# Two real parts instead of three ahead of the first output of layer 0's channel transform

## The chip, the cores and the metric

The kernel runs on one core of one Trainium2 chip. The metric is the device time of one execution in microseconds (us); the time before is the median of three executions, 749.95 us. Beside the times there is one profiled execution with its trace. TensorE is called PE in the profile (its weight loads PEld), VectorE is DVE, ScalarE is ACT, GpSimd is POOL, and SP is the queue from which all of this kernel's DMAs are issued.

## What is computed

Two layers, each a Fourier mixing followed by a linear-attention block, on a 2048 x 640 matrix of 32-bit floats, each part with a layer norm ahead of it and a residual behind it.

```python
def _A_ref(x, dft_seq_re, dft_seq_im, dft_hid_re, dft_hid_im):
    a = jnp.einsum("bsd,ed->bse", x, dft_hid_re)
    b = jnp.einsum("bsd,ed->bse", x, dft_hid_im)
    return jnp.einsum("ts,bse->bte", dft_seq_re, a) - jnp.einsum("ts,bse->bte", dft_seq_im, b)

def _B_ref(x, wqkv, wo):            # B, S, D = 1, 2048, 640; 32 heads of 20
    q, k, v = split_heads(x @ wqkv)
    pq, pk = phi(q), phi(k)         # phi(t) = where(t > 0, t + 1, exp(t)) + 1e-6
    kv, z = pk^T v, sum(pk)         # per head
    return merge_heads((pq @ kv) / (pq . z + 1e-6)) @ wo

for layer in range(2):
    x = x + _A_ref(_layernorm(x), ...)
    x = x + _B_ref(_layernorm(x), B_wqkv, B_wo)
```

## The kernel before

**Tiles and precision.** The 2048 rows are 16 tiles of 128 rows, `X[0]` to `X[15]`, which stay in SBUF throughout. A product is made of three matmuls on a reduced-precision 32-bit type: each operand is split into a high part (a cast, on ACT, line L183) and a low part (source minus high part, line L184, on DVE or POOL), and high by high, high by low and low by high are added up in PSUM.

**The Fourier part.** The matrix is folded by its mirror symmetries, so that the sequence transform is made in classes. `Fourier.whole` (plan word `sCc`) makes one piece of a class: matmuls at L1061 and L1066, then the split of the result, the tiles `u`. The channel transform takes these as stationary operands: `hidden` makes one real or imaginary part of 128 rows from 9 matmuls of 322 columns (L1102). `Fourier.outputs(par, ahead, mid)` (plan word `oPA`) makes the four outputs `r` of one parity. Output `r` needs its real part `real(r)` and its imaginary part in one PSUM tile; `ahead` is the number of real parts that are written before the first imaginary one, and each output then gives out one more. An output is evacuated by ACT (`yi`, L1127 or L1129) and DVE (`ym` at L1130, `yp` at L1131), and four additions put it into two of the row tiles (`lo`, L1133 and L1134; `hi`, L1141 and L1142). The first output of even parity also has one special row, made by another `hidden` into a PSUM tile `p2` and copied at L1138 and L1139.

```python
    def outputs(self, par, ahead, mid=None):
        ...
        for r in range(ahead):
            real(r)
        for r in range(4):
            p = pu[r]
            self.hidden(2 * par + 1, 128 * r, p, 512)
            if r == 0 and mid is not None:
                mid()
            ...                      # yi, ym, yp and the additions into lo
            if par == 0 and r == 0:
                p2 = k.psum()
                self.hidden(0, 512, p2, 0)
            ...                      # the additions into hi
            real(r + ahead)
```

**The plan of layer 0.** `PLANS[0]` is a list of words that are worked through in order by `Fourier.work`: the odd outputs (`o11`), six pieces of classes, `w` (the key weights: five loads into `raw`, five splits into ten tiles `w`), `b` (the first layer norm of the attention, `xn0`, made at L177), `q` (the query weights, five more loads and splits), and `o03t`: the even outputs with three real parts ahead, where the `t` puts `Attention.begun` in as `mid`. `begun` transposes `xn0` on PE (five matmuls, L196, into a PSUM tile) and splits it into `x0` (L183 on ACT, L184 on DVE), which is the stationary operand of the first key and query projections (L245). `keys_values` follows: a loop over the 16 row tiles with one key and one query projection each.

**Buffers.** There are four PSUM tiles of two banks each, taken in turn by real parts, `begun`, `p2` and the projections, 12 buffers `tmp` (the channel weights take six of them, and `xn0`, `x0`, `yi`, `ym`, `yp` come from it too), 4 buffers `raw` for weights and for the tiles `ck` of a check of the input matrices, and 31 buffers for `u`, `w` and others.

**What sets the order.** In this stage the order of instructions on PE, ACT, DVE and POOL is not written by hand. A planner takes at compile time, from the instructions that are ready in its own view of time, the one with the highest priority: the place in the program, moved by the table `AHEAD`. There the query weights' splits have a head start of 200 places (`'0w0': 200`), the evacuation of even output 0 is put back by 600 (`'0out00': -600`), and that of even output 3 is put ahead by 600 (`'0out03': 600`). Each engine then works through its list in order, each instruction waiting for its operands and its buffer. The DMA queue keeps the order of the program. Within `keys_values` the planner also places the steps of the check (L1230, DVE); in the later outputs of layer 0's attention the order is written by hand.

Of the kernel before, what the change touches and what calls it, by code (L numbers as in the profile page):

```python
# [56 lines left out]
ASTATS = ((4, 10, 11, 13, 14), (1, 4, 8, 10))  # L57
VSTATS = ((4, 7, 13), (1, 2, 6, 7, 8, 13, 15))
RESID = ((4, 4), (3, 3))
PLANS = ('o11 s11 s12 s02 s00 s01 s10 w b q o03t', 's00 o12 s11 s12 s10 s01 s02 b w q o01t')  # L60
COL = (0, 1, 3, 2)
WLOWS = ((4, 0), (1, 1))
PAUSES = (4, 10, 11, 12, 13, 14)
# [955 lines left out]
class Fourier:  # L1019
# [141 lines left out]
    def run(self, T, att):  # L1161

        self.work(T, att, PLANS[self.k.layer])

# [370 lines left out]
```

## Time and profile before

| | us |
|---|---|
| median of three executions (749.91 to 750.39) | 749.95 |
| the profiled execution | 750.25 |
| its span in the trace | 748.1 |
| PE busy in the span | 726.5 |
| PE weight loads busy | 690.3 |
| DVE busy | 585.1 |
| ACT busy | 374.5 |
| POOL busy | 248.9 |

The span is what the trace covers from its first to its last instruction; the profiled execution was 2.15 us longer than that. Busy times of different engines overlap. Matmuls are pipelined, and a busy PE counts the modelled length of each, so two of them overlap in part. The granted TensorE clock is 1.00 throughout. In the timeline, a row has the start, the length, the engine, the line, the operation, output and input with their shapes and the count; what stands in brackets is how long the engine was idle ahead of it and what it had waited for.

### The profile page before, as it was taken

Reading aid. Unit: us, or ns where it says so; the run is one execution under the profiler, and the core shown is the slowest. Engines: PE = TensorE matmul, PEld = TensorE weight load, DVE = VectorE, ACT = ScalarE, POOL = GpSimd, SP = SyncE. Lnnn points to the kernel's source line nnn. Section 1 sums busy time; section 2 is a strip of 40 time slices with the busy share of each in tenths; the row PEclk is TensorE's granted clock in tenths of the full one; section 3 lists DMA queues with packets and bytes.
Section 4 is the critical chain, followed back from the end, with each engine's and each line's share of the span. In section 5 each row is a group of like instructions: output and inputs, shape, how many; then the busy total and the mean of one; then the engine's idle time right before and its main releaser. Section 6 shows DMA issues by size and latency. Waiting matters only on the chain.

```text
span 748.1 us, 12737 instructions
## 1 busy us (share of the span) xinstructions
PE 726.5 (97%) x4734; PEld 690.3 (92%) x4734; DVE 585.1 (78%) x1142; ACT 374.5 (50%) x705; POOL 248.9 (33%) x282
## 2 busy tenths in 40 slices
PE   4999999999999999999999999999999999999997
PEld 1388999999999999899986999999999999989997
DVE  7997798758968786888984756966887886689983
ACT  7745655664355543455773336566532554443320
POOL 5237932120014002567773672026000020154300
PEclk9999999999999999999999999999999999999999
DMA  9322467445665840400043222645265535002553
GB/s 335 97 90 90 128 201 257 126 133 181 187 187 184 283 146 21 151 9 1 11 140 133 70 94 77 222 144 168 59 187 168 164 114 155 23 12 71 178 171 114
DMA packets 55548, 98.78 MB, mean 132 GB/s; under 512 B 5268, under 2 KB 22935, under 8 KB 55479
## 3 DMA queue, kind: packets, MB, share of 16 engines
q1 hardware_dynamic: 55479, 97.89, 41.2%
q8 instruction: 39, 0.64, 0.4%
q14 instruction: 30, 0.25, 0.1%
HBM read 75.84 MB, written 21.63 MB: 130 GB/s over the span
## 4 chain that ended last, share of the span: by engine, by line
PE 80%; DVE 10%; ACT 6%; issue 2%; DMA 1%; POOL 1%; SPq 0%; DVEq 0%; ACTq 0%
PE ps L245 50%; PE ps L338 18%; PE ps L1156 4%; PE ps L1102 4%; PE ps L520 2%; PE ps L196 1%; DVE t L184 1%; PE ps L1061 1%; DVE w L184 1%; ACT t L885 1%; DVE ps L586 1%; DVE x L615 1%; ACT t L886 1%; ACT ab L922 1%; ACT ab L923 1%
## 5 line engine op out<-in xcount | busy, mean ns | idle before, releaser
L245 PE MATMUL ps<-w,t 128*128 128x320 f32 x2880 | 432.4, 310 | 0.5 <-DVE w L184 0.2
L245 PEld LDWEIGHTS ps<-w,t 128*128 128x128 f32 x2880 | 422.9, 188 | 2.0 <-DVE t L184 0.4
L338 PE MATMUL ps<-t,t 128*128 128x256 f32 (+1 forms) x640 | 139.9, 309 | 0.0
L1230 DVE CUSTOM_DVE_ANT_0 junk<-ck,ck 128x688 bf16<-128x688 f32 (+5 forms) x138 | 103.6, 751 | 7.5 <-DMA ck<-in_ck 5.7
L338 PEld LDWEIGHTS ps<-t,t 128*128 128x128 f32 x640 | 106.9, 188 | 0.0
L338 PE MATMUL ps<-w,t 128*128 128x384 f32 (+1 forms) x320 | 98.6, 310 | 0.7 <-DVE w L184 0.6
L370 ACT ACTIVATE t<-ps 128x640 f32<-128x640 f32 x64 | 45.1, 704 | 96.3 <-PE ps L245 96.2
L183 ACT CAST t<-t 128x640 fp32r<-128x640 f32 x62 | 45.2, 728 | 68.7 <-DVE t L213 41.1
L570 POOL TENSOR_TENSOR t<-pq,t 128x640 f32<-128x640 f32 x26 | 42.5, 1642 | 106.4 <-ACT t L488 77.3
L407 POOL TENSOR_TENSOR t<-t,s 128x640 f32<-128x640 f32 x16 | 28.4, 1772 | 130.1 <-DVE s L373 123.5
L338 PEld LDWEIGHTS ps<-w,t 128*128 128x128 f32 x320 | 60.2, 188 | 1.4 <-DVE w L184 1.3
L184 DVE TENSOR_TENSOR t<-t,t 128x640 fp32r<-128x640 f32 x52 | 43.3, 833 | 19.5 <-ACT t L183 11.7
L1102 PE MATMUL ps<-t,u 128*128 128x322 f32 x306 | 48.1, 315 | 1.1 <-DVE t L184 1.1
L1102 PEld LDWEIGHTS ps<-t,u 128*128 128x128 f32 x306 | 46.0, 189 | 2.2 <-issue 1.3
L372 ACT ACTIVATE t<-t 128x640 f32<-128x640 f32 x64 | 47.5, 742 | 0.0
L373 DVE SCALAR_TENSOR_TENSOR pq<-t,pq 128x640 f32<-128x640 f32 x32 | 27.6, 863 | 23.9 <-ACT t L372 23.9
L373 DVE SCALAR_TENSOR_TENSOR s<-t,s 128x640 f32<-128x640 f32 x32 | 26.9, 842 | 20.4 <-ACT t L372 20.4
L184 POOL TENSOR_TENSOR t<-t,t 128x640 fp32r<-128x640 f32 x10 | 16.2, 1620 | 71.9 <-ACT t L183 71.8
L183 ACT CAST t<-ps 128x640 fp32r<-128x640 f32 (+1 forms) x36 | 24.8, 690 | 27.2 <-PE ps L196 23.5
L183 ACT CAST t<-s 128x640 fp32r<-128x640 f32 x32 | 23.3, 728 | 29.5 <-DVE t L184 17.4
L1156 PE MATMUL ps<-cw,ab 128*128 128x512 f32 x80 | 35.6, 595 | 1.4 <-ACT ab L922 1.0
L184 DVE TENSOR_TENSOR t<-ps,t 128x640 fp32r<-128x640 f32 (+1 forms) x36 | 29.2, 812 | 7.9 <-ACT t L183 7.9
(198 smaller groups left out, 987.3 us busy)
## 6 DMA issues: line engine op xcount, KB each, us to landing
ck<-in_ck SPq DMA_DIRECT2D x48, 346.0 KB
ck<-in_ck SPq DMA_DIRECT2D x48, 344.0 KB
turn<-t SPq DMA_DIRECT2D x23, 320.0 KB
save<-w SPq DMA_DIRECT2D x20, 320.0 KB
w<-save SPq DMA_DIRECT2D x20, 320.0 KB
z<-turn SPq DMA_DIRECT2D x19, 320.0 KB
x<-in_x SPq DMA_DIRECT2D x16, 320.0 KB
out<-x SPq DMA_DIRECT2D x13, 320.0 KB
```

Source lines behind the costliest of these rows:

```text
L183: self.nc.scalar.copy(hi, src)
L184: return self.engine(pool).tensor_tensor(lo, src, hi.bitcast(F32), op=ALU.subtract)
L245: nc.tensor.matmul(pu[:m, 512 * h : 512 * h + HD], s, w[:, HD * h : HD * h + HD], start=first, stop=last)
L338: nc.tensor.matmul(self.place(G, c, part), x[:, 128 * c : 128 * c + 128], p[:, f : f + n], start=start and i == 0, stop=stop and i == 2, s ...
L370: nc.scalar.activation(h2(e), halves(pu), AF.Relu, scale=-1.0)
L372: nc.scalar.activation(e, e, AF.Exp, scale=-1.0)
L373: k.ve.scalar_tensor_tensor(out, e, 1e-6, out, op0=ALU.add, op1=ALU.add)
L407: k.engine(n not in PKSUMS[k.layer]).tensor_tensor(pksum, pksum, pk, op=ALU.add)
L570: k.behind(k.nc.gpsimd.tensor_tensor(t1, self.PQ[self.order2[n]], self.zb, op=ALU.mult), lull)
L1102: self.k.nc.tensor.matmul(po[:, o : o + 322], s[:, f : f + 128], w[:, x, :], start=start, stop=stop)
L1156: self.k.nc.tensor.matmul(self.sum(j), T.out["o", q][:, 128 * j : 128 * j + 128], self.C[2, g], start=n == 0, stop=n == 3)
L1230: i = nc.vector.tensor_tensor_reduce(k.junk[:, : a.shape[1]], b, a, 1.0, 0.0, op0, op1, o)
```

## The change

The word `o03t` of layer 0's plan becomes `o02t`: two real parts are written ahead of the first imaginary part, in place of three. The third real part is then written after output 0 (and `p2`), and the fourth after output 1. Nothing is added or left out: the same matmuls, transposes, evacuations and loads are made, in another order of the program, which the planner starts from.

```diff
-PLANS = ('o11 s11 s12 s02 s00 s01 s10 w b q o03t', 's00 o12 s11 s12 s10 s01 s02 b w q o01t')
+PLANS = ('o11 s11 s12 s02 s00 s01 s10 w b q o02t', 's00 o12 s11 s12 s10 s01 s02 b w q o01t')
```

## The prediction

> **What bounds the kernel now.** I read the page first, then who made PE wait around the changed stage, then that stage in order of time on each engine, then the stage after it.
>
> ```profile
> span 748.1 us, 12737 instructions
> ...
> PE 726.5 (97%) x4734; PEld 690.3 (92%) x4734; DVE 585.1 (78%) x1142; ACT 374.5 (50%) x705; POOL 248.9 (33%) x282
> ...
> PE 80%; DVE 10%; ACT 6%; issue 2%; DMA 1%; POOL 1%; SPq 0%; DVEq 0%; ACTq 0%
> ```
>
> PE is busy for 97% of the span and carries 80% of the chain that ended last. The change neither adds nor removes an instruction, so a gain can only be a pause of PE that goes away, and a loss only a pause that comes. The waits of PE between 30 and 140 us are two, and one of them lies in the stage that the change reorders:
>
> ```profile
> PE ps L1102 <- DVE t L184: 1.1, 1, 1.1
> PE ps L1156 <- ACT ab L922: 0.2, 1, 0.2
> ```
>
> The timeline of PE there:
>
> ```profile
> 63.66 5.89 PE L1102 MATMUL ps<-t,u 128*128 128x322 f32 x37
> 69.38 0.71 PE L196 MATMUL ps<-ident,t 128*128 128x128 f32 x5
> 69.85 2.78 PE L1102 MATMUL ps<-t,u 128*128 128x322 f32 x17
> 73.69 4.29 PE L1102 MATMUL ps<-t,u 128*128 128x322 f32 x27 [1.06 <-DVE t L184]
> 77.93 6.26 PE L245 MATMUL ps<-w,t 128*128 128x320 f32 x41
> ```
>
> A part is 9 matmuls, and the last 27 take 77.93 - 73.69 = 4.24 us, so 0.157 us for one and 1.41 for a part. There are nine parts, 81 matmuls. The counts (37, 17, 27, one record put into the neighbouring group) read as four parts, the transposes of `begun`, two parts, a pause of 1.06, three parts. With the four PSUM tiles this can be named: real 0, 1, 2 and the transposes fill all four (imaginary 0 goes into the tile of real 0); then only imaginary 1 and 2 have a place; then `p2`, real 3 and imaginary 3 wait until one tile comes back. The bracket says which: the one that the split of `x0` gives back (L184). Why so late is seen on ACT, DVE and POOL:
>
> ```profile
> 64.55 2.61 ACT L183 CAST w<-raw 128x640 fp32r<-128x640 f32 x4
> 69.72 0.73 ACT L183 CAST w<-raw 128x640 fp32r<-128x640 f32 x1 [2.57 <-DMA raw<-in_wqkv]
> 71.36 0.73 ACT L183 CAST w<-raw 128x640 fp32r<-128x640 f32 x1 [0.91 <-DMA raw<-in_wqkv]
> 72.00 0.69 ACT L183 CAST t<-ps 128x640 fp32r<-128x640 f32 x1
> 72.58 0.73 ACT L183 CAST w<-raw 128x640 fp32r<-128x640 f32 x1
> 73.21 0.43 ACT L1129 COPY t<-ps 128x322 f32<-128x322 f32 x1
> ...
> 65.83 3.02 DVE L184 TENSOR_TENSOR w<-raw,w 128x640 fp32r<-128x640 f32 x4
> 70.48 0.82 DVE L184 TENSOR_TENSOR w<-raw,w 128x640 fp32r<-128x640 f32 x1 [1.63 <-ACT w L183]
> 72.72 0.82 DVE L184 TENSOR_TENSOR t<-ps,t 128x640 fp32r<-128x640 f32 x1 [1.41 <-ACT t L183]
> 73.67 0.49 DVE L1130 TENSOR_TENSOR t<-ps,t 128x322 f32<-128x322 f32 x1
> ...
> 72.17 4.86 POOL L184 TENSOR_TENSOR w<-raw,w 128x640 fp32r<-128x640 f32 x3 [3.98 <-DMA raw<-in_wqkv]
> 76.99 1.12 POOL L1134 TENSOR_TENSOR x<-x,t 128x319 f32<-128x319 f32 x1
> ```
>
> The transposes are over at about 70.1, but their cast starts at 72.00: it stands in ACT's list behind the fifth and sixth weight cast, and the sixth waits 0.91 us for its load. Then DVE subtracts (72.72 to 73.54), and PE goes on at 73.69. Output 0's own evacuation stands still later, at 73.21 on ACT.
>
> **The change part by part.**
>
> *The order on PE.* Real 0, real 1 and imaginary 0 now come first. By the first group (36 matmuls in 69.38 - 63.66 = 5.72 us) these 27 end at 67.95, and the transposes at about 68.4, both 1.4 us sooner than before. Their source `xn0` is there by then:
>
> ```profile
> 64.64 0.61 DVE L177 TENSOR_SCALAR t<-x,kept 128x640 f32<-128x640 f32 x1 [0.65 <-POOL kept L158]
> ```
>
> Only three PSUM tiles are held at 68.4, so `p2` has the fourth without a wait (to 69.83), and imaginary 1 follows into the tile of real 1 (to 71.24). From there PE needs a tile given back: 71.24 is the new deadline, with two parts of cover behind the transposes as before, but both of them 1.4 us sooner.
>
> *What meets the deadline.* The stage cut at the gaps of ACT:
>
> ```profile
> 67.20:69.70 2.50, 2.50 (x19) 2.49 (x18) 1.65 (x3) 0.00 (x0) 0.99 (x2) 1.00 0.79 241
> 69.70:72.70 3.00, 2.93 (x21) 2.66 (x19) 0.82 (x1) 2.06 (x4) 0.53 (x1) 1.00 0.79 254
> 72.70:77.90 5.20, 4.21 (x27) 4.06 (x27) 5.05 (x9) 3.67 (x7) 5.20 (x4) 1.00 0.58 181
> ```
>
> Columns are stretch, length, then busy time (and instructions) of PE, PEld, DVE, ACT, POOL. From 67.20 to 69.70 ACT does nothing: it waits for the load of the fifth weight tile. Imaginary 0 (67.95) and the transposes (68.4) end inside that hole. The copy of output 0 (0.43) and the cast of the transposes (0.69) fit into it, to about 69.3; DVE, idle from 68.85 to 70.48, then needs 0.82 for the split or two times 0.49 for output 0, so that a tile is free between 69.9 and 70.7, ahead of 71.24. It hinges on the list: the planner must put this cast ahead of the fifth weight cast, or at least the sixth. In the list of before it stands behind the sixth and ahead of the seventh, although the query weights have the higher priority; so in the planner's view the seventh load was not there when the cast was ready, and the sixth was. Ready 1.4 us sooner, against 71.36 - 69.72 = 1.64 us between the fifth and sixth casts on the chip, it most likely moves up by at least one place. Behind the fifth only, it would end at 71.15 and the split at 72.0: a pause of 0.8 in place of 1.06. Ahead of the fifth, no pause. I take no pause, 1.06 us off, since output 0's copy, ready at 67.95, fills the same hole.
>
> *The bound of that term.* The trace's pause of 1.06 is counted from the modelled end of a matmul.
> The Trainium skill (Perfetto Trace Analysis, Identifying the Most-Contended Engine) says that the busy share of matmuls is a poor measure, since they are pipelined, and that of the weight loads a better one.
> By that rule the gain would be 1.3 us, as the next row shows, and the sum lower by 0.24.
>
> ```profile
> L1102 PEld LDWEIGHTS ps<-t,u 128*128 128x128 f32 x81 | 12.2, 190 | 1.3 <-issue 1.3
> ```
>
> I keep 1.06 and use 1.3 as the lower end.
>
> *What is late next.* Without the pause the nine parts end at 76.87 in place of 77.93, and the first key projection starts there. It needs ten weight tiles (the fifth pair was there at 71.3) and a PSUM tile; real 0, the transposes, real 1 and `p2` come back by then, and real 2 and 3 take two of them. So this start is covered. The second key projection is closer:
>
> ```profile
> 81.36 1.74 ACT L171 ACTIVATE t<-x,nb,kept 128x640 f32<-128x640 f32 x2 [2.91 <-POOL x L1142]
> 86.35 0.81 DVE L184 TENSOR_TENSOR t<-ps,t 128x640 fp32r<-128x640 f32 x1
> 84.88 15.84 PE ps L245 x108
> ```
>
> From the chain's row, 108 matmuls take 15.84 us, 0.147 each; the first query has 18 left at 84.88, so the second key starts at 87.52, and its operand is split at 86.35 + 0.81 = 87.16. The margin is 0.36. Ahead of that split ACT stood idle 2.91 us for a buffer that POOL's addition at L1142 gave back. If POOL's list stays as it is, PE keeps 0.36 of the 1.06 and waits the rest here; if output 0's additions go into POOL's own hole (the 3.98 us ahead of 72.17), they give buffers back over 1 us sooner, and all 1.06 stays. I take the middle, 0.7.
>
> *The rest.* No DMA is issued in the moved code, so the queue's list is as before; its loads into `raw` may start sooner or later with the splits that give the buffers back. POOL's list holds the last split of a query weight and its predecessors (1.62 us each, 4.86 for three), among which output 0's additions may now stand:
>
> ```profile
> 78.07 2.17 POOL L184 TENSOR_TENSOR w<-raw,w 128x640 fp32r<-128x640 f32 x1
> 63.25 0.73 DVE L184 TENSOR_TENSOR u<-ps,u 128x512 fp32r<-128x512 f32 x2
> ```
>
> The first row ends at 80.24; the first query, 30 matmuls of 0.147 behind 76.87, starts at 81.3 and still finds it, with 1 us of cover. The second row is the last large split of a class ahead of the stage, over at 63.98, while imaginary 0 now starts two parts behind 63.66, at 66.5.
>
> **Sum.** 750.25 for the profiled execution, less 0.7, is 749.55; the median of the runs is 0.30 below the profiled execution, so 749.25, given as 749.3. Its own range is 748.6 (1.3 off, all kept) to 750.0 (nothing kept). A measurement of this kernel tells about 0.2%, 1.5 us, from no change; so this forecast is no change.
>
> **The rivals.**
>
> *The split stays behind the sixth cast.* Then the tile comes back at 73.69 as before, but PE runs out at 71.24: a pause of 2.45 in place of 1.06, 1.39 us more, 751.3. For it: the query weights' head start in the priorities. Against it: the empty stretch of ACT above.
>
> *The lists behind the stage change (the slower side).* Key and query projections, check steps and splits are put in order by the same planner, which now starts from other times. The place is DVE in the key loop, which has no slack in its first stretch:
>
> ```profile
> 100.00:120.00 20.00, 20.00 (x139) 20.00 (x139) 19.22 (x37) 11.00 (x18) 2.57 (x4) 1.00 0.88 268
> L1230 DVE CUSTOM_DVE_ANT_0 junk<-ck,ck 128x688 bf16<-128x688 f32 (+5 forms) x138 | 103.6, 751 | 7.5 <-DMA ck<-in_ck 5.7
> ```
>
> A check instruction takes 0.751 us. One that newly stands ahead of a split for which PE is due costs about that, once the margin (0.36 above) is used. One undoes the gain of 0.7; three net make it slower by over 0.2%; five give 5 x 0.751 - 0.7 = 3.06, so 753.0; eight give 755.3. For it: DVE is busy for 19.22 of 20 us, and PE hardly waits in this loop now, so there is more to lose than to win. Against it: where DVE has a backlog, its order follows priorities rather than small shifts of time, and these are unchanged.
>
> *The lists change for the better.* The waits of PE in the whole run on splits:
>
> ```profile
> PE ps L245 <- DVE t L184: 1.9, 3, 1.5
> PE ps L245 <- DVE w L184: 1.0, 2, 0.8
> PE ps L338 <- DVE w L184: 0.6, 1, 0.6
> ```
>
> Together 3.5 us. Half of them gone and 0.7 from the stage would be 2.45 off, 747.5.
>
> *The change does nothing.* The planner might place real 2 ahead of imaginary 0 all the same, since it takes what is ready: 749.95. Against it: imaginary 0 now comes first in the program, and its operand is split 2.5 us before (the row above).
>
> **How the numbers follow.** Forecast 0.37, split behind the sixth cast 0.13, lists worse 0.37, lists better 0.09, nothing 0.04. Faster by over 0.2% is the better lists and a little of the forecast's lower end: 0.10. Slower is most of the worse lists (0.35) and 0.05 of the late split, which lies at the bound: 0.40. The rest, 0.50, is within 0.2%. The likeliest case gives 749.3. The range 748.0 to 755.0 takes in the forecast's own range, the late split and up to seven check instructions; outside lie half of the better lists and the tail of the worse, some 0.13.
>
> **What would show it.** Right: PE's first group at L1102 has 27 matmuls, the transposes stand near 68; on ACT the copy at L1129 and the cast of the transposes come ahead of the fifth or sixth weight cast; no wait of PE on L184 stands between 63 and 77, and the first projection starts near 76.9. If the second key starts at 87.5 as before, the margin took the gain. The late split shows as one pause of 2.4 us near 71. The worse lists show as new waits of PE at L245 or L338 between 90 and 320 us, and the prediction is wrong if these, or PE waits in the second layer, sum to over 2 us.

## The result, and the profile after

The median went from 750.2 us to 747.75 us: a ratio of 0.9971, with a 95% interval of 0.996 to 0.9981. That is 2.45 us, 0.29%, just beyond the 0.2% that a measurement here can tell. A second comparison gave 747.42 us and 0.9961 (0.9946 to 0.9976). The forecast was 749.3 us, within 0.2% of no change, with a range from 748.0: the right side and the right pause, but too small a gain, and 0.25 us below the range. The profiled execution took 747.61 us, against 750.25 before.

The page of the kernel after: span, PE's busy time, the chain.

```profile
span 745.8 us, 12737 instructions
...
PE 725.0 (97%) x4734; PEld 689.2 (92%) x4734; DVE 586.4 (79%) x1142; ACT 374.5 (50%) x705; POOL 246.9 (33%) x282
...
PE 16%; DVE 1%; ACT 0%; issue 0%; ACTq 0%
```

The same number of instructions is done in 2.3 us less. The chain's line is not comparable with the one before: here it could be followed back through 17% of the span only. PE's timeline in the changed stage after (start, length, engine, line, what, count):

```profile
63.42 3.05 PE L1102 MATMUL ps<-t,u 128*128 128x322 f32 x18
66.31 0.71 PE L196 MATMUL ps<-ident,t 128*128 128x128 f32 x5
66.77 9.67 PE L1102 MATMUL ps<-t,u 128*128 128x322 f32 x63
76.28 6.29 PE L245 MATMUL ps<-w,t 128*128 128x320 f32 x42
```

No row has a bracket: the pause is gone. The first group has 18 matmuls, two parts, so the transposes stand behind real 1 and *ahead* of imaginary 0, earlier than forecast. From the first part to the first key projection it is 76.28 - 63.42 = 12.86 us, where it was 14.28 (63.66 to 77.93, before rounding). ACT and DVE after:

```profile
64.32 2.61 ACT L183 CAST w<-raw 128x640 fp32r<-128x640 f32 x4
67.11 0.69 ACT L183 CAST t<-ps 128x640 fp32r<-128x640 f32 x1 [0.18 <-PE ps L196]
70.20 0.73 ACT L183 CAST w<-raw 128x640 fp32r<-128x640 f32 x1 [2.40 <-DMA raw<-in_wqkv]
70.84 0.42 ACT L1129 COPY t<-ps 128x322 f32<-128x322 f32 x1
...
68.55 0.81 DVE L184 TENSOR_TENSOR t<-ps,t 128x640 fp32r<-128x640 f32 x1
70.97 0.82 DVE L184 TENSOR_TENSOR w<-raw,w 128x640 fp32r<-128x640 f32 x1 [1.60 <-ACT w L183]
```

The cast of the transposes now runs at 67.11, ahead of the fifth weight cast, which waits 2.40 us for its load. So the split ends at 68.55 + 0.81 = 69.36. PE, with imaginary 0, `p2` and imaginary 1 behind the transposes (27 matmuls of (76.28 - 66.77) / 63 = 0.151 us), comes to the next part at 66.77 + 4.08 = 70.85 and finds the tile.

The orders of instructions of PE, DVE, ACT and POOL differ between the two kernels only inside this stage and the first key and query projections; the queue's order is the same, and nothing behind was put in another order. Between 80 and 110 us the weight loads of after wait twice, where those of before have no wait:

```profile
PEld ps L245 <- DVE t L184: 0.3, 1, 0.3
PEld ps L245 <- ACT t L183: 0.2, 1, 0.2
```

They belong to the second key projection. The rows of its operand after:

```profile
80.47 1.74 ACT L171 ACTIVATE t<-x,nb,kept 128x640 f32<-128x640 f32 x2 [2.29 <-DVE t L1131]
...
84.94 0.69 ACT L183 CAST t<-ps 128x640 fp32r<-128x640 f32 x1
...
86.31 0.81 DVE L184 TENSOR_TENSOR t<-ps,t 128x640 fp32r<-128x640 f32 x1
```

It is split at 87.12, as late as before (87.16), while PE now comes to it earlier.

Cut at the same instructions, the traces read as in this table (us, worked out from starts in PE's timeline before rounding). The cuts are the first even part, the first key projection, the transposes of the third operand, the first matmul of the Gram products (L520) and layer 1's first at L1156. "Again" is another execution of the same kernel in another comparison.

| stretch | before | before again | after | after again | one real part ahead | one, again | after, three POOL splits |
|---|---|---|---|---|---|---|---|
| up to the first even part | 63.66 | 63.40 | 63.42 | 63.67 | 63.66 | 63.49 | 63.39 |
| changed stage | 14.28 | 14.53 | 12.86 | 12.86 | 13.08 | 13.08 | 12.86 |
| first two keys | 22.62 | 22.57 | 23.09 | 23.55 | 22.49 | 22.49 | 22.50 |
| up to L520 | 192.83 | 192.57 | 192.34 | 192.54 | 192.47 | 192.74 | 192.47 |
| up to layer 1's L1156 | 94.16 | 94.13 | 93.81 | 93.82 | 94.29 | 94.30 | 93.85 |
| the rest | 360.51 | 360.83 | 360.26 | 360.04 | 360.59 | 360.66 | 360.18 |

By the means of two executions each, before and after, the stage gives 1.55, the first keys take back 0.72, and three later stretches, in which no instruction was moved, give 0.26, 0.33 and 0.52. So the moved instructions account for 0.8 us, less than half of the gain.

### The profile page after: what moved, and what is told of

Its sections match the earlier page's. It is cut to its first block, busy times and chain, and to the rows that moved or that the text cites. A ratio compares the mean times of both kernels' runs of the same rounds, so it can differ in the third digit from the quotient of the medians.

```text
span 745.8 us, 12737 instructions
## 1 busy us (share of the span) xinstructions
PE 725.0 (97%) x4734; PEld 689.2 (92%) x4734; DVE 586.4 (79%) x1142; ACT 374.5 (50%) x705; POOL 246.9 (33%) x282
## 5 line engine op out<-in xcount | busy, mean ns | idle before, releaser
L1156 PE MATMUL ps<-cw,ab 128*128 128x512 f32 x80 | 35.6, 595 | 2.2 <-ACT ab L923 1.4
L158 POOL TENSOR_TENSOR kept<-ve,mhalf 128x1 f32<-128x1 f32 x32 | 21.8, 699 | 41.4 <-DVE ve L157 40.1
```

The costliest lines, as they stand in the source:

```text
L1156: self.k.nc.tensor.matmul(self.sum(j), T.out["o", q][:, 128 * j : 128 * j + 128], self.C[2, g], start=n == 0, stop=n == 3)
```

## The experiments

Theory 1: the pause is a shortage of the four PSUM tiles, and it goes when the tile of the transposes comes back before PE runs out. Rivals: it goes only through the sooner split, whatever the number of parts; or only through the number of parts; or the gain is not in this stage at all.

**The transposes first, three parts ahead.** In layer 0 the order of the program becomes `begun`, then imaginary 0; three real parts stay ahead.

```diff
-            self.hidden(2 * par + 1, 128 * r, p, 512)
-            if r == 0 and mid is not None:
-                mid()
+            first = [mid] if r == 0 and mid is not None else []
+            for step in (first + [lambda: self.hidden(...)])[:: -1 if k.layer else 1]:
+                step()
```

> Three real parts ahead as before the change, but in the program the transposes of the first operand stand ahead of imaginary part 0 (layer 0 alone). The instruction lists differ from those before the change in this stage alone; the cast of the transposes moves up by one place, between the fifth and the sixth weight cast. Theory 1 (the split of the transposes comes too late on ACT): PE has imaginary 0, 1 and 2 as cover, to about 72.6 us, and the split is done at about 72.0; the pause of 1.06 us goes, first key projection 1.2 to 1.4 us sooner, time 748.5 to 749.1. Rival 1 (what counts is that one real part less holds a PSUM tile, so that p2 has one): four tiles are held as before, the pause stays, 750.2. Rival 2 (what counts is that output 0 is evacuated sooner): output 0 is no sooner here, 750.2.

Measured: 749.74 us, ratio 0.9984 (0.9973 to 0.9995); the profiled execution, 751.33 us, was the slowest of its twelve. Its PE timeline:

```profile
68.24 0.71 PE L196 MATMUL ps<-ident,t 128*128 128x128 f32 x5
68.71 5.18 PE L1102 MATMUL ps<-t,u 128*128 128x322 f32 x33
74.26 2.93 PE L1102 MATMUL ps<-t,u 128*128 128x322 f32 x18 [0.37 <-ACT t L1129]
77.58 6.40 PE L245 MATMUL ps<-w,t 128*128 128x320 f32 x42 [0.39 <-DVE t L1131]
...
89.35 0.86 PE L245 MATMUL ps<-w,t 128*128 128x320 f32 x4 [1.01 <-DVE t L184]
```

The wait for the split in the stage is gone, but two others stand in its place, for the tiles of the first outputs (L1129, L1131), and the second key waits 1.01 us. The stage is 14.02 us, 0.26 shorter than before. A sooner split alone moves the wait to the next tile: my expectation, the whole pause gone and 748.5 to 749.1 us, fell.

**Two parts ahead, the transposes late.** The change, with each matmul of `begun`'s transposes in layer 0 tied behind the last matmul of imaginary 0, which is the order that the prediction had assumed (the diff is shown in part). PE's timeline then has 29 matmuls ahead of them, the 27 of these parts and two more.

```diff
-        self.x0 = self.k.split_chunks(self.k.transposed(self.xn0))
+        tp = self.k.transposed(self.xn0)
+        [self.k.behind(t, self.k.last) for t in self.k.tps if self.k.part == 0 and not self.k.general]
+        self.x0 = self.k.split_chunks(tp)
```

> Two real parts ahead as after the change, but the transposes are tied behind the last matmul of imaginary part 0, where the program has them. In the lists the cast of the transposes falls back by one place, behind the fifth weight cast. Theory 1: PE has p2 and imaginary 1 as cover, to about 71.1 us; the fifth weight cast ends at 70.9, so the cast at 71.6 and the split, behind that weight's split on DVE, at 72.6; a pause of 1.2 to 1.8 us comes back, 749.0 to 749.7. Rival 1 (one real part less) and rival 2 (output 0 sooner): both are as after the change, 747.8 within 0.3.

Measured: 749.9 us, ratio 0.9987 (0.9976 to 0.9998). PE and ACT:

```profile
67.91 0.71 PE L196 MATMUL ps<-ident,t 128*128 128x128 f32 x5
68.38 2.64 PE L1102 MATMUL ps<-t,u 128*128 128x322 f32 x16
72.09 5.66 PE L1102 MATMUL ps<-t,u 128*128 128x322 f32 x36 [1.07 <-DVE t L184]
...
69.72 0.73 ACT L183 CAST w<-raw 128x640 fp32r<-128x640 f32 x1 [2.84 <-DMA raw<-in_wqkv]
70.35 0.69 ACT L183 CAST t<-ps 128x640 fp32r<-128x640 f32 x1
```

This is the prediction's hinge, on the chip. The transposes are over near 68.6, when ACT has nothing to do, yet their cast stands in the list behind the fifth weight cast and waits with it for the load. The pause is back with 1.07 us, and the stage has 14.20 us. The transposes' place on PE, behind 29 matmuls (67.91) or behind 18 (66.31), decides on which side of that cast the planner puts this one. The pause came out shorter than I expected (1.2 to 1.8), and the time still above the 749.0 to 749.7 that I gave.

**Three parts ahead, the cast on DVE.** The kernel before, with the high part of the transposes made by DVE in place of ACT; the orders of PE, POOL and the queue stay. The flag `on_dve` is set for layer 0's `begun` alone (lines left out here).

```diff
-        self.nc.scalar.copy(hi, src)
+        (self.nc.vector.tensor_copy if self.on_dve else self.nc.scalar.copy)(hi, src)
```

> Before the change, but the cast of the transposes (layer 0 alone) is made by DVE, right ahead of its subtraction, in place of ACT; the lists of PE, POOL and the DMA queue are those before the change, ACT's lacks the one cast. Theory 1: the split waits for no load of the sixth weight any more; cast and subtraction stand behind the fifth weight's split on DVE (ends at 71.3), so done at about 72.9 in place of 73.54: the pause falls from 1.06 to about 0.4, 749.5. Rivals 1 and 2: PE's order and output 0's are unchanged, 750.2 within 0.2.

Measured: 749.51 us, ratio 0.9984 (0.9972 to 0.9996). PE and DVE:

```profile
69.28 7.15 PE L1102 MATMUL ps<-t,u 128*128 128x322 f32 x44
77.14 6.40 PE L245 MATMUL ps<-w,t 128*128 128x320 f32 x42 [0.70 <-ACT t L1129]
...
69.54 0.83 DVE L184 TENSOR_TENSOR w<-raw,w 128x640 fp32r<-128x640 f32 x1 [1.26 <-ACT w L183]
70.28 0.82 DVE L183 CAST t<-ps 128x640 fp32r<-128x640 f32 x1
```

The cast no longer stands behind the sixth weight cast; on DVE it still follows the split of the fifth weight. The pause at the split is gone, of which I had expected 0.4 us to stay; but 0.70 us turns up ahead of the first key, which waits for a tile that ACT's copy of an output gives back. The stage is 14.05 us. So ACT's list was the reason for *that* wait, and with three parts ahead the next tile is nearly as late. The time is the 749.5 us that I expected, by another wait than I expected.

**One real part ahead.** `o03t` becomes `o01t`.

> One real part ahead of the first output in place of two. The transposes come on PE behind the first 9 matmuls, the cast behind the second weight cast. Theory 1: there is no pause left to win, the split only comes still sooner; the transposes want the normalised row tile at 65.0, just when PE comes to them, so 0 to 0.4 us may be lost: 747.7 to 748.3. Rival 1 (each real part less gives a gain): another 1 us off, 746.7. Rival 2 (output 0 sooner): it is sooner by one part, up to 0.6 off since buffers come back sooner ahead of the second key projection, 747.2.

Measured: 748.69 us, ratio 0.998 (0.9967 to 0.9992), and in a second comparison 748.21 us, 0.9971 (0.9962 to 0.998). PE:

```profile
63.66 1.70 PE L1102 MATMUL ps<-t,u 128*128 128x322 f32 x9
65.38 0.74 PE L196 MATMUL ps<-ident,t 128*128 128x128 f32 x5
65.87 11.03 PE L1102 MATMUL ps<-t,u 128*128 128x322 f32 x72
76.74 6.28 PE L245 MATMUL ps<-w,t 128*128 128x320 f32 x42
```

There is no pause here either. The stage is 13.08 us, 0.22 longer than with two, since 9 matmuls last until 65.1 and the source of the transposes is made by DVE only near 65.2 (64.64 + 0.61 in the row of L177, before). The first keys take 22.49 us: no loss there. By the moved instructions alone two would thus have no advantage over one: 0.22 in the stage, less the 0.60 to 1.06 that the stretch of the first two keys costs it. The medians say otherwise. In the comparison with both, one took 748.21 us and two 747.42, and the difference lies in the later stretches. The first measurement was above the 747.7 to 748.3 us that I expected.

**Both kernels again.** Before against itself: 750.25 us, ratio 1.0001 (0.999 to 1.0013).

> The kernel before once more, against itself, to see what of the difference between the two traces is the change and what differs from one execution to the next. If the stretches outside the changed stage (the start, 0.24 us; the fold behind layer 0's attention, 0.35 us; the second layer) differ by the execution, this trace shows differences of 0.2 to 0.5 us there and the stage itself at 14.3 us again (first even part to first key projection); ratio 1.000 within 0.001.

> The kernel after once more. Theory 1 (the stage alone): the stage takes 12.9 us again in place of 14.3, the second key projection loses 0.5 to 0.6 again, about 0.4 of that is won back at the first Gram product, and nothing else repeats: 1.4 us off, ratio 0.9981. Rival (the change also makes later stretches shorter): the fold behind the attention is 0.35 shorter again, ratio 0.997.

> One real part ahead, once more, beside the kernel after on the same chip. Theory 1: the stage takes 13.1 us, 0.2 more than with two, as PE reaches the transposes before their row tile is normalised, but nothing is lost at the second key projection, since the split of the second operand came 1.5 us sooner; from the stage to the third operand's transposes 0.4 us less than with two, so a ratio 0.0005 below that of the kernel after. Rival (what the first look showed): 0.0009 above it.

The pause in the second execution of before, with ACT's sixth weight cast, and then the stage and the third operand in the second execution of after:

```profile
73.69 4.28 PE L1102 MATMUL ps<-t,u 128*128 128x322 f32 x27 [1.32 <-DVE t L184]
...
71.37 0.73 ACT L183 CAST w<-raw 128x640 fp32r<-128x640 f32 x1 [1.28 <-DMA raw<-in_wqkv]
```

```profile
67.02 9.67 PE L1102 MATMUL ps<-t,u 128*128 128x322 f32 x63
76.53 6.29 PE L245 MATMUL ps<-w,t 128*128 128x320 f32 x42
...
PE ps L196 <- DVE t L177: 0.9, 1, 0.9
```

The same kernel's pause reads 1.06 in one execution and 1.32 in another. The rows say why: the sixth weight cast, which waits for its load, starts at 71.36 and 71.37, so PE goes on at 73.69 in both, while PE had come to the stage 0.26 sooner in the second (63.40 against 63.66). An earlier PE only waits longer here. In its second execution the kernel after does not wait at the second key; it loses 0.9 us at the third operand's transposes instead. The stage's 12.86 us comes again to the hundredth. The ratios went with the rival of both expectations, that the later stretches get shorter too: two parts are at 0.9961, not at the 0.9981 of the stage alone, and one part is 0.0010 above two, not 0.0005 below.

**The changed kernel, a weight split off POOL.** Of the query weights' low parts POOL makes three in place of four, DVE one more; the orders of PE, ACT and the queue are the same as after.

```diff
-WLOWS = ((4, 0), (1, 1))
+WLOWS = ((3, 0), (1, 1))
```

> Two real parts ahead, and the last of the four query-weight splits that POOL makes is made by DVE instead. The lists of PE, ACT and the DMA queue are those after the change. It bears on the 0.59 us that the kernel after loses at the second key projection: ACT's norm of the second row tile and its evacuation of the first key wait there for temporary buffers that output 0's and 1's additions on POOL hold. If POOL's backlog is the cause, its additions come 1.6 us sooner and the loss goes: the way from the first key to the third operand's transposes takes 22.5 in place of 23.1 us. Against it: on DVE the split stands ahead of the evacuation of output 1 (yp) and waits for its cast, which may hold the PSUM tile for the first key projection by 0.5 us; then the stage takes 13.4 and the sum is unchanged.

Measured: 747.82 us, ratio 0.9971 (0.9959 to 0.9983); its span of 745.3 us is the shortest of the profiled executions, but its median is not to be told from after's. PE, and the second key's operand on ACT and DVE:

```profile
66.74 9.67 PE L1102 MATMUL ps<-t,u 128*128 128x322 f32 x63
76.25 6.29 PE L245 MATMUL ps<-w,t 128*128 128x320 f32 x42
...
79.06 0.93 ACT L171 ACTIVATE t<-x,nb,kept 128x640 f32<-128x640 f32 x1 [1.12 <-DVE t L1131]
...
84.88 0.81 DVE L184 TENSOR_TENSOR t<-ps,t 128x640 fp32r<-128x640 f32 x1
```

The operand's split starts 1.43 us sooner than after (84.88 against 86.31), the first two keys take 22.50 us, and no weight load between 80 and 110 us waits. The loss behind the stage was thus that of late operands. That POOL's list alone made them late is not shown: in this execution the fifth weight cast came 0.47 us sooner already (69.73 against 70.20), ahead of all that the edit moves. And the second execution of after, with the lists of the first, splits the operand at 85.80 and has no wait at the second key. The last weight split on DVE and POOL's split beside it, in the first execution of after and then in the second:

```profile
77.56 2.01 DVE L184 TENSOR_TENSOR w<-raw,w 128x640 fp32r<-128x640 f32 x1 [1.67 <-ACT w L183]
77.33 1.56 POOL L184 TENSOR_TENSOR w<-raw,w 128x640 fp32r<-128x640 f32 x1
```

```profile
77.56 0.82 DVE L184 TENSOR_TENSOR w<-raw,w 128x640 fp32r<-128x640 f32 x1 [1.36 <-ACT w L183]
77.63 2.18 POOL L184 TENSOR_TENSOR w<-raw,w 128x640 fp32r<-128x640 f32 x1
```

Where POOL's split had begun first, DVE's took 2.01 us in place of 0.82 and ended 0.68 behind it (79.57 against 78.89); where DVE's began first, POOL's took 2.18 in place of 1.56. Behind that split on DVE stands L1131, which gives back the buffer that ACT's L171 waits for (80.47 above). So POOL's start, 0.23 us before DVE's or 0.07 behind it, went with a difference of 1.2 us ahead of L1131, of which 0.5 is left at the operand's split. Why the two take turns here no run tests.

**The later stretches.** The stretch that ends at layer 1's L1156 lies at 93.81, 93.82 and 93.85 us in the three executions with two parts ahead and the early transposes, and at 93.90 to 94.30 in seven others. Where the time goes can be named. DVE's waits there, first before, then after, then one part ahead:

```profile
DVE ab L964 <- ACT ab L963: 0.9, 1, 0.9
```

```profile
DVE ab L964 <- ACT ab L963: 0.6, 1, 0.6
```

```profile
DVE ab L964 <- ACT ab L963: 0.6, 1, 0.6
DVE ps L586 <- POOL ab L933: 0.5, 1, 0.5
```

The wait at L964 is 0.28 longer (0.86 against 0.58) in both of before's executions only; the one at L586, 0.47 or 0.48, comes with the transposes first, the late transposes and both executions with one part. The stretch goes with these two waits: 93.81 to 93.90 without either, 94.13 and 94.16 with the first, 94.25 to 94.30 with the second. It does not go with the number of parts: the late transposes have two and 94.25, the cast on DVE has three and 93.90. Why the waits come is open. It is not the time at which the stretch begins: "one part" and "after" both begin it at 291.7 us (the sums of the rows above) and differ by 0.48. The second layer's part ("the rest") is 360.04 to 360.26 in the same three executions with two parts and 360.51 to 360.94 in the seven others; no cause was found for it, and no experiment addressed one.

## Why the prediction was right, and where it was not

*The pause and its cause* were right: four PSUM tiles, and a cast that stands behind a weight cast which waits for its load. The late transposes show the cast behind the fifth weight cast and the pause back; after has it ahead, and none.

*The order on PE* was wrong. It had imaginary 0 ahead of the transposes and these at 67.95; they came at 66.31. I took imaginary 0 as ready since its operand was split on the chip. The planner goes by its own view of time, in which that was presumably not so (this is argued, not shown). With the order as predicted the planner puts the cast behind the fifth weight cast, and no pause is saved: the case that the prediction had priced at 0.8 us of pause, with the split over at 72.0. The chip showed 1.07 and PE going on at 72.09. So the forecast of "no pause" came true by an order that it had not foreseen: in this step it was luck.

*ACT's hole.* The cast lies in it, as said; output 0's copy does not. It stands at 70.84, behind the fifth weight cast. That cost nothing: PE has no wait behind it in the stage.

*The size of the pause* is the term that was mis-sized: 1.06, with 1.3 as the bound, where the stage came out 1.42 shorter (1.67 against before's second execution). Three things are in it: matmuls start 0.151 us apart, so the 17 ahead of the pause end their turn at 69.85 + 2.57 = 72.42, and the gap to 73.69 is 1.27; the first key's weight load had waited another 0.2 before, which also went; and the bracket itself varies, 1.06 to 1.32, between executions. The waits of the weight loads before, between 60 and 80 us:

```profile
PEld ps L1102 <- issue: 1.3, 1, 1.3
PEld ps L245 <- ACT t L1129: 0.2, 1, 0.2
```

The Trainium skill (Perfetto Trace Analysis, Identifying the Most-Contended Engine) takes the busy share of weight loads for a better measure than that of matmuls.
Carried over to a single pause, as the prediction did, it gives 1.3, and the measured 1.42 is nearer to that than to 1.06.

*What is late next* was right in place for the profiled execution: the second key, with its operand split as late as before. The forecast had it take 0.36 of the 1.06. The stretch of the first two keys took back 0.47 there (23.09 - 22.62) and 0.93 in the second execution, where it was the third operand that came late, of which the prediction says nothing. The buffer that ACT waits for is now given back by DVE (L1131), and no longer by POOL's addition (L1142), from whose place the forecast had taken its two cases.

*The lists behind the stage* were not changed. The heaviest rival, at a chance of 0.37, and its better twin both fell: DVE's order in the key loop is the same, as the argument against the rival had it. The twin's 747.5 us lies nearest to the measured time, but by chance: the waits of PE that it would have shortened sum to 3.6 us after, against 3.5 before. The heaviest rival is also what stretched the range upward, to 755.0, while the measurement fell 0.25 us below its lower end.

*The sum.* The stage and the first two keys alone give 1.42 - 0.47 = 0.95 off the profiled execution, near the forecast's 0.7. The other 1.3 us of the span (0.24 ahead of the stage, 1.1 behind) lie where nothing was moved, and they are what carries the time out of the range. The 0.24 is from the execution, since before's second run starts the stage as early. Of the rest, some 0.3 to 0.5 up to L1156 and as much in the second layer came again in each of the three executions with two parts and the early transposes: measured, not explained, and not in any step of the prediction.

## What to carry to other kernels

When tiles run short, find who must give back the *next* one too: with three parts ahead, taking away one holder's delay moved the wait to the next holder in both kernels that tried it (0.37 and 0.39 us, and 0.70), and only the combination (fewer tiles taken ahead, and the early cast) paid. Where a planner orders the engines, read a hinge in the lists that it makes rather than in the chip's times: a step ready in an idle engine's gap still waits if it was listed behind an instruction that waits for a load. Profile each kernel more than once before explaining less than 0.5 us.

## What the runs showed that was not expected

A stretch of 94 us whose instructions were in the same order came out at 93.81 to 93.90 us in four executions and at 94.13 to 94.30 in six, by whether one of two waits of DVE came; two kernels that begin it at the same time differ by 0.48. A pause at one place with the same order read 1.06 and 1.32 us, because its end is set by a load that came at the same time (73.69 in both) and only its start moved. And one and the same split on DVE took 0.82 or 2.01 us in two executions of one kernel, by whether POOL's split beside it had begun first.
